# Five long products in place of 94 small unread ones at the start, and 56 small ones with one long one ahead of N

## The chip, the cores and the metric

The kernel runs on one core of a Trainium2 chip. The metric is the device time of one execution in microseconds; three runs of the kernel before took 701.88, 702.68 and 706.95 us (median 702.68). A separate execution was taken by the profiler; all durations below come from it.

## The reference

For 4 batches and 8 heads, a delta-rule recurrence over 768 tokens of 48 values each; its output, with the heads side by side (384 values a token), goes through a SwiGLU block with 1536 inner columns.

```
k_n = k / (norm(k) + 1e-6)
for t in range(S):
    y[t]  = q[t] @ state
    v_old = k_n[t] @ state
    state = state + beta[t] * outer(k_n[t], v[t] - v_old)
x = y as (B*S, H*D)                       # 3072 x 384
out = (silu(x @ w_gate) * (x @ w_val)) @ w_out
```

Everything is float32.

## The kernel before

The tokens are cut into 12 chunks of 64. Within a chunk the recurrence is turned into matrix products: the chunk's keys and queries are transposed on TensorE (`turned`, L497), Gram matrices of keys with keys and of queries with keys are formed (`first_gram`, L656 and L657, for the first two chunks; `gram_steps`, L513, for the rest), a triangular system is solved by substitution on VectorE, and `advance` applies the result to the values and to the running state (L899, L908, L938, L958, L994, L1006 and others). The feed-forward block of a finished chunk is worked off in between: L1270 for the first two chunks, L1174 for the others, L1380 for the output product. The products of the recurrence are small (64 or 32 rows, 48 to 64 columns) and come in groups of 64 and more; those of the feed-forward block are 128 x 128 with 128 to 256 columns. The order on every engine is written out by hand: the schedule is manual for TensorE, ACT, DVE, SP and POOL, and each engine works through its program in that order.

The change concerns the first chunk pair. Its order on TensorE is: `unread()`, then the transposes of chunk 0's keys, the first Gram, the transposes of chunk 1's keys, sixteen small products that spread beta (`spread_beta`, L438), the second Gram; then transposes and Grams for the first two query chunks and for key chunks 2 and 3. DVE meanwhile computes the norms and, once ACT has copied the second Gram's diagonal blocks (`first_diag`, L662) and DVE has transposed them (L1649), runs the first substitution (L698 and L704, until 27 us), from which `first_z` and `spread_z` (L708, L717, L719) make the tile `zt`. Then `warm(3)` (L644), three products of 512 columns that nobody reads, stands on TensorE ahead of N: `n_products` (L728), called by the first step of `advance(0)`, multiplies `zt` with the lower blocks.

`unread()` forms 94 products of a 32 x 32 block of the constant tile `half` with one column of it (L638); they go to a PSUM bank that nobody reads before it is written again. They wait only for the memset of `half` (L311). A float32 product shows up in the profile as two weight loads and two matmuls, so these are 188 and 188 instructions, and the three products of `warm(3)` are 6 and 6. Both functions take the pair of PSUM banks with the tag "px", which the key Grams of chunks 0 and 2 use too.

Of the kernel before, what the change touches and what calls it, by code (L numbers as in the profile page):

```python
# [15 lines left out]
R = 32  # L16
# [4 lines left out]
def kernel(  # L21
# [25 lines left out]
    nc = tc.nc  # L47
# [21 lines left out]
    def ps_pair(name, tag):  # L69

        return psum.tile([128, 2, 512], FP32, name=name, tag=tag, bufs=1)
# [70 lines left out]
    def load_k(c, dmas=(nc.sync,)):  # L142
        load_heads(kn_of(c), k, c, dmas)

    def load_q(c):
        load_heads(qpad[c % QB], q, c)
# [28 lines left out]
    def load_v(c):  # L175
        vin[c] = work.tile([128, 2, NB, NJ, D], FP32, name="vin", bufs=2)
        for b in range(2):
            src = halves(v, c, b).rearrange("bp (j par) p d -> par p (bp j) d", par=2)
            for par in range(2):
                s = 64 * (b ^ par)  # L180
                nc.sync.dma_start(
                    out=vin[c][s : s + 64, par].rearrange("p bp j d -> p (bp j) d"),
                    in_=src[par],
                )
# [125 lines left out]
    half = const.tile([128, R], FP32, name="half")  # L310
# [46 lines left out]
    def new_n(g):  # L357

        n_t[g] = work.tile([128, 2, HH], FP32, name="n_t")
# [58 lines left out]
    def load_beta():  # L418
        for s_ in range(2):
            for par in range(2):  # L420
                at = beta_rows(s_).start + 8 * par
                nc.gpsimd.dma_start(
                    out=beta_s[at : at + 8],
                    in_=beta.rearrange(
                        "(b bp) (j par) s -> b par (bp j) s", b=2, par=2
                    )[s_ ^ par, par],
                )
# [119 lines left out]
    def gram(*args):  # L547
        for _ in gram_steps(*args):
            pass
# [58 lines left out]
    def first_tiles():  # L608
        a = work.tile([128, C * 2 * HH], FP32, name="a_sb")
        for c in range(2):  # L610
            l_sb[c] = a[:, R * R * c : R * R * (c + 1)].rearrange(
                "p (h k) -> p h k", k=C
            )
        first_of["flat"] = new_mb().rearrange("p k i -> p (k i)")
        first_of["diag"] = first_of["flat"].rearrange("p (j h) -> p h j", j=R)
        first_of["zb"] = places["z1"].bitcast(FP32)[:, 4 * H_ - 1056 : 4 * H_]
        first_of["mb"] = places["wo"].bitcast(FP32)[:, 2 * H_ : 2 * H_ + 1056]
        nc.vector.memset(first_of["zb"], 0.0)
        for c in range(2):
            nc.vector.memset(l_sb[c][:, :, 48:C], 0.0)  # L620
        for x, rows in enumerate((slice(16, C), slice(R, C), slice(48, C), slice(0, R))):
            nc.vector.tensor_reduce(
                out=m_two[:, x],
                in_=ident.rearrange("p (b n) -> p b n", b=2)[:, :, rows],
                axis=mybir.AxisListType.X,
                op=ALU.add,
            )
        nc.vector.tensor_tensor(
            out=m_rows, in0=m_two[:, :, 0], in1=m_two[:, :, 1], op=ALU.add
        )  # L630
        nc.vector.tensor_scalar_mul(m_low, m_rows[:, 0:3], -1.0)

    def unread():

        p = ps_pair("p_t", "px")[:, 0]
        for n in range(94):
            q_ = QUADS[n % 4][0]
            nc.tensor.matmul(p[q_, 0:1], half[q_], half[q_, 0:1])  # L638

    def warm(count):  # L640

        p = ps_pair("p_t", "px")[:, 0]
        for _ in range(count):
            nc.tensor.matmul(p, ident, kts[0][:, 0:512])  # L644
# [15 lines left out]
    def first_diag(c, p):  # L660
        to = first_of["diag"][:, HH * c : HH * c + HH]
        nc.scalar.copy(to.rearrange("p (par h) j -> p par h j", par=2), p[:, :, 1])  # L662
# [957 lines left out]
    with tc.manual_schedule(  # L1620
        engines={
            mybir.EngineType.PE,
            mybir.EngineType.Activation,
            mybir.EngineType.DVE,
            mybir.EngineType.SP,
            mybir.EngineType.Pool,
        }
    ):
        new_n(0)
        load_beta()  # L1630
        first_tiles()
        norms(0)
        norms(1)
        load_q(0)
        load_k(2)
        load_k(3)
        load_q(1)
        load_v(0)
        copy_a = nc.scalar.copy
        unread()  # L1640
        turned(0, False, 0)
        p_g = [first_gram(0, "px")]
        first_diag(0, p_g[0])
        turned(1, False, 2)
        spread_beta(copy_a)
        p_g.append(first_gram(1, "py"))
        first_diag(1, p_g[1])
        r_b = first_n()
        nc.vector.transpose(first_of["mb"][:, 0 : R * R], first_of["flat"])  # L1649
        first_scale(r_b)  # L1650
        for n in range(12):
            stage(n, n - 2 if n > 1 else None)
        load_v(1)
        stage(12, 10)
        stage(13, 11)
        low_copies(0, p_g[0])
        turned(0, True, 0)
        low_copies(1, p_g[1])
        turned(2, False, "px")
        first_q = [gram_steps(0, True, 2)]  # L1660
        next(first_q[0])
        turned(3, False, "py")
        turned(1, True, 0)
        gram(2, False, "px", (copy_a, copy_a))
        gram(3, False, "py", (copy_a, copy_a))
        first_q.append(gram_steps(1, True, 0))
        next(first_q[1])
        for n in (0, 2):
            power_step(n)
        first_substitution()  # L1670
        for n in range(14, 18):
            stage(n, n - 3)
        first_z()
        for n in range(18, 23):
            stage(n, n - 3)
        some, others = slice(0, HH // 2), slice(HH // 2, HH)
        spread_z(0, 1, nc.scalar, some)
        spread_z(0, 0, nc.vector)
        spread_z(0, 1, nc.vector, others)
        scale_v(0)  # L1680
        for steps_of in first_q:
            next(steps_of)
        warm(3)
        new_nt(0, qpad[1].rearrange("p bp h d -> p (bp h d)"))
        zb_1 = work.tile([128, R, R], FP32, name="zb", bufs=1)
        new_nt(1, zb_1.rearrange("p k i -> p (k i)"))
        step("advance", advance, 0)
        for x in range(2):
            spread_z(1, x, nc.scalar)
        for n in (4, 1, 3, 5, 6, 7):  # L1690
            power_step(n)
        for _ in range(6):
            step("advance", advance, 0)
        converts_first(0)
        step("advance", advance, 0)
        converts_first(2)
        p_n = banks("p_n", "px")
        n_products(1, p_n, (0,))
        step("advance", advance, 0)
        converts_first(4)  # L1700
        n_products(1, p_n, (1,))
        converts_first(1, 3)
        converts_first(5)
        scale_v(1)
        for par in range(2):
            n_copy(1, p_n, par)

        def chain(at):

            step("advance", advance, 0 if steps("advance", 0) < 4 else 1)  # L1710
            converts(1 + (at + 1) % 2)

        pairs = [(c, f) for c in range(2) for f in range(0, 8, 2)]
        pairs += [(c, f) for f in range(8, FT, 2) for c in range(2)]
        for at, (c, f) in enumerate(pairs):
            early = c == 0 and f < 4
            if c == 1 and f == 0:
                finish(1)
                second_inverse.append(invert(1))
                for _ in range(3):  # L1720
                    next(second_inverse[0])
            elif not early:
                point(2)
            need((6, 12, 18, 24, 30, 30)[f // 2])
            gate_val(c, f, fill, at, chain if early else None)
        need(len(pieces))
        for bp in range(NB):
            point(2)
            output(0, bp, fill, (4, 8))
        output(1, 0, fill, (4, 8))  # L1730
        hold.clear()
        first_blocks(True)
        first_blocks(False)
        point(2)
        output(1, 1, fill, range(2, FT, 2))
        finish(2)
        x_sums(2)
        sums_of_w(12)
        for c in range(2, NCH):
            if c > FAST:  # L1740
                begin(c, 0)
            point(c + 1)
            if c == FAST:
                begin(c, 0)
            for r in range(ROUNDS):
                gate_val_fast(c, r, fill)
            output_fast(c, fill)
            finish(c + 1)
            x_sums(c + 1)
# [30 lines left out]
```

## Time and profile before

| | |
|---|---|
| three runs, median | 702.68 us |
| profiled execution, its own time | 704.07 us |
| its span, first to last instruction | 702.4 us |
| TensorE busy (matmul / weight load) | 684.1 / 643.0 us |
| VectorE, ScalarE, GpSimd busy | 473.0, 259.4, 54.0 us |
| mean granted TensorE clock in the records | 0.994 |
| first transposes (L497), first start | 5.71 us |
| N (L728), first start | 31.88 us |

The table's first three rows are times of whole executions: the profiled one took 1.7 us more than its span, and 1.4 us more than the median. Busy times are sums of instruction durations without their overlap. In the lines of the prediction, L followed by a number is a line of the kernel, PE stands for TensorE's matmuls and PEld for its weight loads; "idle before" names what ended the wait of an engine. "issue" is idle time for which the profile shows no other engine or transfer.

### The profile page before, as it was taken

The page shows a single profiled execution, that of the slowest core. Times are in us where ns is not written, and L with a number is a line of the kernel's source. Part 1 is how long each engine was busy: PE and PEld are TensorE (multiplying, and loading weights), DVE is VectorE, ACT ScalarE, POOL GpSimd, SP SyncE. Part 2 cuts the span into 40 slices and gives each one's busy share as a digit, 9 for nine tenths or more (in the row PEclk, how much of TensorE's full clock was granted, in tenths as well). Part 3 has the DMA queues.
Part 4 walks back from the last instruction along what each step waited for, and adds up shares of the span by engine and source line. Part 5 has one row for each costly group of instructions (what it writes and reads, how often), then busy time and mean ns, then how long its engine had stood idle before and what let it go on. Part 6 is the DMA issues. An engine that isn't in the chain of part 4 may idle for free.

```text
span 702.4 us, 25797 instructions
## 1 busy us (share of the span) xinstructions
PE 684.1 (97%) x11450; PEld 643.0 (92%) x11450; DVE 473.0 (67%) x1103; ACT 259.4 (37%) x542; POOL 54.0 (8%) x62
## 2 busy tenths in 40 slices
PE   6899999999999999999999999999999999999997
PEld 5788888757999989999999999999999999999997
DVE  6786788798899738887468787379844345333342
ACT  4674865214442523244223235232153132142220
POOL 4110031105000120000300000200000000000000
PEclk9999999999999999999999999999999999999999
DMA  8578724017450621365333264143241131221210
GB/s 133 155 183 210 215 85 141 4 37 174 126 108 13 118 69 46 77 130 91 75 84 72 56 133 88 31 117 84 55 107 48 42 84 59 55 62 46 68 46 23
DMA packets 143855, 62.33 MB, mean 89 GB/s; under 512 B 122976, under 2 KB 126048, under 8 KB 143744
## 3 DMA queue, kind: packets, MB, share of 16 engines
q1 hardware_dynamic: 141536, 60.19, 36.3%
q8 instruction: 90, 1.47, 0.8%
q10 hardware_dynamic: 2080, 0.39, 0.4%
q0 software_dynamic: 128, 0.10, 0.1%
q14 instruction: 21, 0.17, 0.1%
HBM read 53.58 MB, written 7.08 MB: 86 GB/s over the span
## 4 chain that ended last, share of the span: by engine, by line
PE 95%; ACT 2%; issue 1%; DVE 1%; DMA 1%; ACTq 0%; DVEq 0%
PE ffn L1174 43%; PE ffn L1380 20%; PE ffn L1270 9%; PE ffn L1297 4%; PE p_g L513 3%; PE p_u L938 2%; PE p_r L899 2%; PE p_s L1006 2%; PE p_y L908 2%; PE p_y L994 1%; PE p_f L1067 1%; PE p_u L958 1%; PE ffn L958 1%; PE ffn L497 1%; PE p_j L876 1%
## 5 line engine op out<-in xcount | busy, mean ns | idle before, releaser
L1174 PE MATMUL ffn<-x_ffn,wg_sb 128*128 128x128 f32 x840 | 128.9, 276 | 0.4 <-ACT x_ffn L1073 0.2
L1174 PE MATMUL ffn<-x_ffn,wv_sb 128*128 128x128 f32 x840 | 128.5, 276 | 0.0
L1174 PEld LDWEIGHTS ffn<-x_ffn,wg_sb 128*128 128x128 f32 x840 | 111.7, 193 | 0.6 <-ACT ffn L1230 0.3
L1174 PEld LDWEIGHTS ffn<-x_ffn,wv_sb 128*128 128x128 f32 x840 | 111.1, 193 | 0.1
L1204 ACT ACTIVATE sil<-ffn 128x256 f32<-128x256 f32 x120 | 46.1, 384 | 133.6 <-PE ffn L1174 125.3
L1380 PE MATMUL ffn<-wo_sb,h_f 128*128 128x192 f32 x480 | 83.4, 327 | 0.0
L1209 DVE TENSOR_TENSOR h_f<-sil,ffn 128x256 f32<-128x256 f32 x120 | 49.6, 418 | 49.5 <-ACT sil L1204 47.2
L1380 PEld LDWEIGHTS ffn<-wo_sb,h_f 128*128 128x128 f32 x480 | 78.1, 190 | 0.4
L1341 DVE TENSOR_TENSOR ffn<-ffn,p_sb 128x512 f32<-128x512 f32 x58 | 40.3, 695 | 44.3 <-ACT ffn L1230 43.2
L1174 PE MATMUL ffn<-x_t,h_f 128*128 128x128 f32 x480 | 61.0, 280 | 0.2 <-ACT ffn L1187 0.2
L1174 PEld LDWEIGHTS ffn<-x_t,h_f 128*128 128x128 f32 x480 | 56.2, 191 | 1.4 <-ACT ffn L1187 0.4
L591 DVE TENSOR_TENSOR zb<-zb,tmp 128x31 f32<-128x31 f32 (+15 forms) x155 | 53.1, 343 | 5.3
L585 DVE TENSOR_TENSOR tmp<-zb,mb 128x31 f32<-128x31 f32 (+15 forms) x155 | 52.7, 340 | 4.0
L807 POOL TENSOR_TENSOR n_b<-mb,half 128x32 f32<-128x32 f32 x5 | 30.0, 6003 | 294.6 <-DVE mb L555 294.6
L1341 DVE TENSOR_TENSOR o_sb<-o_sb,ffn 128x192 f32<-128x192 f32 x49 | 17.2, 352 | 51.2 <-PE ffn L1380 49.1
L1187 ACT COPY ffn<-ffn 128x512 f32<-128x512 f32 x30 | 17.1, 571 | 63.7 <-PE ffn L1174 57.3
L1380 PE MATMUL ffn<-last_k,h_f 128*128 128x192 f32 x200 | 35.9, 327 | 0.0
L1270 PE MATMUL ffn<-x_ffn,wg_sb 128*128 128x256 f32 x144 | 34.4, 385 | 0.0
L1270 PE MATMUL ffn<-x_ffn,wv_sb 128*128 128x256 f32 x144 | 33.8, 382 | 0.0
L1380 PEld LDWEIGHTS ffn<-last_k,h_f 128*128 128x128 f32 x200 | 32.9, 190 | 0.0
L1174 PE MATMUL ffn<-x_ffn,p_sb 128*128 128x128 f32 x216 | 30.9, 287 | 0.0
L1270 PEld LDWEIGHTS ffn<-x_ffn,wg_sb 128*128 128x128 f32 x144 | 26.5, 190 | 4.4 <-DVE wg_sb L304 0.8
(289 smaller groups left out, 1070.0 us busy)
## 6 DMA issues: line engine op xcount, KB each, us to landing
h_f<-w_s SPq DMA_DIRECT2D x60, 256.0 KB, 2.7
p_sb<-w_s SPq DMA_DIRECT2D x27, 256.0 KB, 2.9
vin<-in_v_dram SPq DMA_DIRECT2D x48, 96.0 KB, 3.0
out_dram<-o_sb SPq DMA_DIRECT2D x48, 96.0 KB, 2.2
kn<-in_k_dram SPq DMA_DIRECT2D x20, 192.0 KB, 4.8
zt<-in_moe_w_out_dram SPq DMA_DIRECT2D x6, 384.0 KB, 3.7
qpad<-in_q_dram SPq DMA_DIRECT2D x36, 64.0 KB, 2.9
w_s<-h_f SPq DMA_DIRECT2D x7, 256.0 KB, 4.3
```

The source lines that it names most:

```text
L513: nc.tensor.matmul(p_v[par][half_of(b if of_q else b ^ par), bp, j], kt[c][half_of(par), bp, j, b], xt[half_of(par), bp, j, b],)
L585: nc.vector.tensor_tensor(out=t_v, in0=zb[:, 0 : j + 1, j : j + 1].to_broadcast([128, j + 1, m]), in1=mb[:, j : j + 1, j + 1 : R].to_broad ...
L591: nc.vector.tensor_tensor(out=zb[:, 0 : j + 1, j + 1 : R], in0=zb[:, 0 : j + 1, j + 1 : R], in1=t_v, op=ALU.add,)
L807: nc.gpsimd.tensor_tensor(out=n, in0=mb.rearrange("p j i -> p (j i)")[:, 0 : R * R : R + 1], in1=half, op=ALU.pow,)
L1174: nc.tensor.matmul(p[:, u], w(u), moving, start=start and u == 0, stop=True, skip_group_check=True,)
L1187: nc.scalar.copy(p_y, p_x)
L1204: nc.scalar.activation(sil[:, n].rearrange("p (i n) -> p i n", i=2), p[:, 0:2], ACTF.Silu)
L1209: nc.vector.tensor_tensor(out=h_of(c, f, j), in0=sil[:, n].rearrange("p (i n) -> p i n", i=2), in1=p[:, 2:4], op=ALU.mult,)
L1270: nc.tensor.matmul(ps[name][:, i], w_sb[:, t, (f + i) * 128 : (f + i + 1) * 128], xts[c][:, t], start=(t == 0 and i == 0), stop=(t == KT - 1),
L1297: nc.tensor.matmul(p_o, hs[c, f - f % 2][:, f % 2, bp * 128 : (bp + 1) * 128], wo_sb[:, f], start=(f == 0), stop=(f == FT - 1),)
L1341: nc.vector.tensor_tensor(out=out, in0=a, in1=b, op=ALU.add)
L1380: nc.tensor.matmul(p[x, part], a(f - f % 2)[:, f % 2], b(f), start=not begun and f == 0, stop=f == FH - 1, skip_group_check=True,)
```

## The change

`unread` gets a count and forms products of the whole 128 x 32 tile `half` with one of its columns broadcast to 512; it is called with 5. The old small products become `small_unread(count)`, called with 56 behind the first query Grams. `warm` is called with 1 instead of 3. Nothing else is different.

```diff
-    def unread():
+    def unread(count):
 
         p = ps_pair("p_t", "px")[:, 0]
-        for n in range(94):
+        for _ in range(count):
+            nc.tensor.matmul(p[0:R], half, half[:, 0:1].to_broadcast([128, 512]))
+
+    def small_unread(count):
+
+        p = ps_pair("p_t", "px")[:, 0]
+        for n in range(count):
             q_ = QUADS[n % 4][0]
             nc.tensor.matmul(p[q_, 0:1], half[q_], half[q_, 0:1])
...
-        unread()
+        unread(5)
         turned(0, False, 0)
...
         for steps_of in first_q:
             next(steps_of)
-        warm(3)
+        small_unread(56)
+        warm(1)
         new_nt(0, qpad[1].rearrange("p bp h d -> p (bp h d)"))
```

## The prediction, made before the changed kernel ran

> **What bounds the kernel now.** I read the page's engine table and its chain first: is there any engine but TensorE to gain from?
>
> ```profile
> PE 684.1 (97%) x11450; PEld 643.0 (92%) x11450; DVE 473.0 (67%) x1103; ACT 259.4 (37%) x542; POOL 54.0 (8%) x62
> PE 95%; ACT 2%; issue 1%; DVE 1%; DMA 1%; ACTq 0%; DVEq 0%
> q8 instruction: 90, 1.47, 0.8%
> ```
>
> TensorE carries the end; what the change can touch is its idle time, the "issue" share and its clock. Next the waits of TensorE's matmuls from 33 us on, after the edited start:
>
> ```profile
> PE p_j L876 <- issue: 2.4, 2, 1.6
> PE p_y L908 <- issue: 1.2, 1, 1.2
> PE p_y L994 <- issue: 0.8, 1, 0.8
> ```
>
> The three longest sums are put down to no engine. Then TensorE's timeline in the edited stretch (start, length, instructions; in brackets the idle time before and what ended it), and one line of the chain there:
>
> ```profile
> 1.03 2.98 PE L638 MATMUL p_t<-half 32*32 32x1 f32 x188 [1.03 <-DVE half L311]
> ...
> 28.38 0.80 PE L513 MATMUL ffn<-qt,kt 64*64 64x64 f32 x35 [1.90 <-issue]
> 29.11 2.84 PE L644 MATMUL p_t<-kt,ident 128*128 128x512 f32 x6
> ```
>
> ```profile
> 31.95 1.14 PE p_n L728 x64
> ```
>
> 94 small products are 188 loads and 188 matmuls; they end at 4.01, and the first real work (L497) starts at 5.71, when its keys land. The three long products (L644) stand directly ahead of N (L728). Last, the view by windows around the longest late stall (stretch, length, busy time of TensorE, weight load, DVE, ACT and POOL, then clock, DMA share, GB/s):
>
> ```profile
> 248.59:250.15 1.56, 0.00 (x1) 0.00 (x0) 0.00 (x0) 0.00 (x0) 1.42 (x2) 1.00 0.00 0
> 250.62:254.03 3.41, 3.41 (x17) 3.41 (x18) 1.22 (x1) 0.96 (x1) 0.00 (x0) 0.50 0.18 53
> ```
>
> TensorE stands for 1.56 us; the next 3.41 us run at clock 0.50.
>
> To find what "issue" is I numbered TensorE's records by start. The stalls that end at 13.33, 28.38, 51.44, 165.49, 170.04, 245.05, 250.15 and 349.53 all fall on number 193 modulo 256. Queue q8 brings 90 packets of 16 KB, and 90 x 256 is 23,040, about TensorE's 23,053 records: q8 is its program. At each of these stalls the next block starts 1.3 to 1.5 us after its packet ends (packet 25.95 to 26.89, restart 28.38), and nowhere in the trace sooner. So **TensorE stalls for its own instructions** where a run of small products eats 256 instructions (2.0 to 3.6 us) faster than a block arrives: the packet starts 0.9 to 2.3 us after the previous block is entered, takes 0.9 to 1.5, and needs another 1.4.
>
> **What the Trainium skill says.** "Runtime: NRT & Kernel Launch", section Instruction fetch mechanics: blocks of 16 KiB (256 instructions) are fetched by the sequencer's own DMA queue, the cost "mostly hidden". The block size agrees; the hiding fails here for 1 to 2 us at a time. "TensorE: Matmul & The Clock Gate", Part 1: the array runs at half rate until a window of some 3.4 us was busy, and falls back after an idle one; the windows run freely. The trace agrees: a 128-column transpose takes a median 421 ns from 5.7 to 11.5 us and 272 at 22 us; the clock records begin with full at 11.69, and half windows last 3.41 us (18.51, 250.62). The page's clock of 1.00 before 11.69 is the absence of a record.
>
> **The change part by part.** No step of another engine moves: SP, POOL, ACT and DVE issue the same instructions and DMAs. TensorE's program changes in length.[...] Out: 94 x 4 = 376. In: 5 x 4 = 20, then 56 x 4 = 224. Of `warm`, 12 become 4. Up to the small ones everything is 356 earlier in the program, from N on 140.
>
> *Start.* At full clock L644's matmuls start 0.45 us apart (29.11 to 31.36, five steps). At half clock L497 took 1.94 us for 8 matmuls against 1.03, a factor 1.9: 0.85 us apart. Ten from 1.03 on end at 9.5 if the clock never rises. If 3.4 us of them count as a busy window, it rises between 4.4 and 7.85, by the phase; then they end at 1.03 + 4 x 0.85 + 6 x 0.45 = 7.1 up to 8.75. With this trace's phase (11.69 less 2 x 3.413 = 4.86): 7.3. They block L497, ready at 5.71, and all behind it on TensorE: **1.4 to 3.0 us late**. At full clock it regains 0.9 in each of two groups of transposes (1.94 and 1.85 against 1.03) and some 0.7 in the first Gram (7.6 to 10.0): 2.5. But the first block that must be fetched now begins 104 instructions into the second Gram; its fetch starts only when the first Gram is half done (about 9.8) and lands at 9.8 + 1 to 2 + 1.4 + 1.4 = 13.6 to 14.6. The last 152 instructions (6.7 ns each: 256 took 1.7 us from 13.33) end the Gram at 14.6 to 15.6 against 15.04. DVE's L1649, which waits for its copy, could start no earlier than 14.92 anyway, when DVE ends L453. Sum: **0** (from -0.6 to +1.2).
>
> *Before N.* The stall from 26.48 lay inside the second query Gram. The boundary is now 40 instructions into the small ones, so the Gram ends unstalled near 26.6 and the stall, until about 28.3, falls into filler. 184 small instructions at 7.9 ns (376 in 2.98 us) take 1.45, the long one 0.9: N at 30.7 instead of 31.9. Its values (`zt`, L717 and L719) are there from 29.2. But the next boundary lies 68 instructions into N; its block, asked for at 28.3, is there at 31.7 to 32.6. N then ends at 32.2 to 33.1 against 33.08: **-0.5** (-2 to +1; the upper end if small products don't hold the clock and a half window, 1.7, follows). The bank px, which the small ones take first, was read last by L539, done at 27.2: no new wait. If the filler were too short, N would wait for `zt`, 29.2.
>
> *Boundaries after N.* They move by 140 instructions. Gaps at old boundaries after 33 us: 1.40, 0.14, 0.34, 0.98, 0.32, 1.75, 1.05 = 6.0 us. I took these out of the trace's starts and replayed the fetches ([...]request to packet constant, 1.0 for the packet, 1.4 to use). With 1.6 us to the packet it returns 4.5 us on the old boundaries, at six of those seven places and a few others; on the new ones **2.3**. With 1.3: 1.1 and 0.8; with 2.0: 9.7 and 4.9; with latencies drawn from the trace's own 4.8 and 3.2. I take 3 left of 6: **-3.0** (-5 to +1). TensorE's waits for other engines after 33 us are 0.7 us at most, so little is swallowed.
>
> *Clock.* No new boundary lies between 240 and 259. Without the 1.56 us stall the window to 250.62 should hold enough work, and 3.41 us at half clock give back half: **-1.7** (0 if the small joins alone starve the window).
>
> Sum: 0 - 0.5 - 3.0 - 1.7 = -5.2. The profiled execution took 704.07 (span 702.4 and 1.7 around it): 698.9. The median shown, 702.68, is 1.4 below that execution: 697.5. **I forecast 698.0.**
>
> **The rivals.**
> *More is gained.* Fetches are quick after 33 us and hardly any stall is left, and the start gains too: -6.0 - 1.7 - 2.0 = -9.7, 693. For it: with 1.3 us to the packet the replay leaves only 0.8. Against it: near 35, 42 and 159 the replay finds new fast blocks while the weights' DMAs load the queues.
> *The stalls only move.* As much stall elsewhere, and a half window after another join: only -0.5 is left, 702. For it: the later joins (L876) are just such runs of small products. Against it: after 27 us, 28 blocks last under 5 us without stalls on the old boundaries, 22 on the new.
> *Slower: the long products stay cold.* Their stationary is 32 columns wide; if such work doesn't raise the clock, they hold L497 until 9.5. From L497 to the end of the second Gram took 9.3 us with its 0.7 stall; 9.5 + 8.6 = 18.1 against 15.04, +3.1, and DVE's substitution carries it to N. With stalls that only move: 705.8; with two more half windows, 709 or more. It decides once they end later than about 8.5.
> *No effect*, the filler being hidden: excluded by the shifted program for the late stalls, but possible in sum, as in the second rival.
>
> **Numbers.** Main case 0.55 (694.5 to 701); more gained 0.25; stalls only move 0.12; cold 0.08. Within 1% (7 us) is what a measurement of this kernel can't tell from no change. Faster by more: the second case and some of the main one, 0.40; same 0.53; slower 0.07. Range 693 to 704: it leaves out about 0.1 on each side.
>
> **What would show it.** Right: L638 with five products ending near 7 to 8; transposes near 280 ns right after; the "issue" stall behind L513 gone from that line and standing in the small products; stalls of L876, L908 and L994 smaller; no half clock after 250. Wrong: transposes still at 421 ns; L497 later than 9; stalls of 1 to 2 us at other lines with the same sum; a half window at 32.

## The result, and the profile after

The changed kernel took 698.88 us (median of 20 runs, 696.57 to 703.43), the kernel before 702.65 us (20 runs, 699.65 to 706.95): a ratio of 0.995, 95% interval 0.9932 to 0.9967. Its profiled execution took 697.91 us over a span of 696.2, against 704.07 over 702.4 before. So the gain is 3.8 us by the medians and 6.2 us between the two profiles; where the other 2.4 us went is taken up below.

From the profile's page of the kernel after: the busy time of each engine, the shares of the chain that ended last, and the queue that carries TensorE's program:

```profile
PE 684.1 (98%) x11380; PEld 638.6 (92%) x11380; DVE 473.2 (68%) x1103; ACT 259.4 (37%) x542; POOL 53.3 (8%) x62
PE 96%; ACT 1%; issue 1%; DVE 1%; ACTq 0%; DVEq 0%
q8 instruction: 89, 1.46, 0.8%
```

TensorE has 70 matmuls and 70 weight loads fewer, 140 instructions, and its program comes in 89 packets instead of 90. Its busy time is the same to a tenth of a microsecond, but by coincidence: up to 33 us it is busy for 27.75 us where it was 25.19, the five long products alone taking 6.62 us for the 2.98 of the 94 small ones, so behind 33 us it is busy for 2.6 us less. The waits of its matmuls from 33 us on (line, waited for: us in total, times, longest):

```profile
PE ffn L964 <- ACT v L953: 0.6, 1, 0.6
PE ffn L964 <- issue: 0.5, 1, 0.5
PE p_t L497 <- ACT x_ffn L1079: 0.4, 1, 0.4
PE p_y L914 <- issue: 0.4, 1, 0.4
PE ffn L1180 <- ACT ffn L1236: 0.2, 1, 0.2
PE p_j L791 <- issue: 0.2, 1, 0.2
```

The lines have moved by 6 (L876 of before is L882, L908 is L914, L994 is L1000). The 2.4 us at the join (L876) and the 0.8 at L994 are gone, the 1.2 at L908 is 0.4. Numbered as in the prediction, the gaps at block boundaries after 33 us sum to 2.4 us, against 6.1 in the kernel before (a gap is the time from the start of one record to the start of the next; those over 0.12 us that end within 1.8 us of a packet's end count). The largest now are 0.68 at 35.85 and 0.62 at 162.70.

Seen by windows, the two stretches where the long late stalls stood (stretch, length, then busy time and instructions of TensorE, weight load, DVE, ACT and POOL, clock, DMA share, GB/s), first before:

```profile
240.00:260.00 20.00, 18.39 (x489) 17.71 (x488) 9.94 (x17) 5.82 (x11) 6.33 (x2) 0.91 0.34 75
345.00:365.00 20.00, 19.14 (x448) 18.53 (x448) 10.26 (x21) 5.97 (x11) 4.74 (x3) 1.00 0.37 89
```

and after:

```profile
240.00:260.00 20.00, 20.00 (x564) 19.50 (x566) 11.10 (x21) 6.98 (x13) 6.58 (x3) 1.00 0.40 92
345.00:365.00 20.00, 20.00 (x451) 19.48 (x450) 12.34 (x28) 6.21 (x13) 0.24 (x1) 1.00 0.33 79
```

TensorE is busy throughout and its clock is full. A half window below is a stretch of 3.41 us for which the records show a clock of 0.50. To see where the time came from I set the records of the two traces side by side by their number counted from the end of the program. The same work is 0.8 us earlier in the kernel after at 55 us, 1.0 at 158, level at 165, 1.5 earlier from 180 to 242, 5.1 at 259, 6.2 from 362 to the end. Between 242 and 259 us 3.6 us are gained in one place: the stalls there (0.32 and 1.75 in the kernel before) and the half window behind them.

The edited stretch, on TensorE's timeline of the kernel after:

```profile
1.03 6.62 PE L637 MATMUL p_t<-half 128*32 128x512 f32 x10 [1.03 <-DVE half L311]
7.58 1.09 PE L497 MATMUL ffn<-ident,kn 128*128 128x128 f32 x8
...
25.88 0.29 PE L644 MATMUL p_t<-half 32*32 32x1 f32 x14
27.67 0.97 PE L644 MATMUL p_t<-half 32*32 32x1 f32 x98 [1.49 <-issue]
28.73 1.59 PE L650 MATMUL p_t<-kt,ident 128*128 128x512 f32 x2
30.25 2.49 PE L734 MATMUL p_n<-zt,a_sb 64*64 64x64 f32 x62
```

Five long products end at 7.6, and the transposes behind them run at full clock: 8 in 1.09 us where they took 1.94. The stall that stood in the query Gram now stands in the small products. N starts 1.6 us earlier than before, but takes 2.5 us instead of 1.2: a block boundary lies in it, and nearly all of it falls into a half window from 29.26 to 32.67 us. The copies behind it (L739) start at 32.87 against 33.11. So the change leaves as many half windows as there were: ahead of the end of the program the profile before has them at 18.51 and 250.62, the one after at 15.61 and 29.26, and the mean granted clock is 0.994 in both. The first 33 us by windows, before and after (the third number from the end is the clock):

```profile
0.00:33.00 33.00, 25.19 (x846) 21.11 (x850) 25.64 (x74) 16.34 (x32) 10.59 (x29) 0.95 0.76 145
0.00:33.00 33.00, 27.75 (x795) 18.85 (x796) 25.31 (x74) 16.37 (x33) 11.06 (x29) 0.90 0.77 137
```

### The profile page after: what moved, and what is told of

The parts are those of the page before. It is cut to its first block, busy times and chain, and to the rows that moved or that the text cites. A ratio compares the mean times of both kernels' runs of the same rounds, so it can differ in the third digit from the quotient of the medians.

```text
span 696.2 us, 25657 instructions
## 1 busy us (share of the span) xinstructions
PE 684.1 (98%) x11380; PEld 638.6 (92%) x11380; DVE 473.2 (68%) x1103; ACT 259.4 (37%) x542; POOL 53.3 (8%) x62
## 3 DMA queue, kind: packets, MB, share of 16 engines
q8 instruction: 89, 1.46, 0.8%
## 4 chain that ended last, share of the span: by engine, by line
PE 96%; ACT 1%; issue 1%; DVE 1%; ACTq 0%; DVEq 0%
PE ffn L1180 43%; PE ffn L1386 20%; PE ffn L1276 9%; PE ffn L1303 4%; PE p_g L513 3%; PE p_u L944 2%; PE p_s L1012 2%; PE p_r L905 2%; PE p_y L914 2%; PE p_y L1000 1%; PE p_f L1073 1%; PE p_t L637 1%; PE ffn L964 1%; PE p_u L964 1%; PE p_j L868 1%
## 5 line engine op out<-in xcount | busy, mean ns | idle before, releaser
L1180 PEld LDWEIGHTS ffn<-x_ffn,wv_sb 128*128 128x128 f32 x840 | 110.7, 192 | 0.0
L1276 PEld LDWEIGHTS ffn<-x_ffn,wv_sb 128*128 128x128 f32 x144 | 27.0, 190 | 3.7
```

What stands on the lines that cost most here:

```text
L1180: nc.tensor.matmul(p[:, u], w(u), moving, start=start and u == 0, stop=True, skip_group_check=True,)
L1276: nc.tensor.matmul(ps[name][:, i], w_sb[:, t, (f + i) * 128 : (f + i + 1) * 128], xts[c][:, t], start=(t == 0 and i == 0), stop=(t == KT - 1),
```

## The experiments

The theory: the gain comes from where the 256-instruction blocks of TensorE's program begin. The rivals: the early warm-up of the clock, the shorter filler ahead of N, or simply fewer instructions. None of the kernels below changes what is computed. Ratios are to the kernel before, timed on the same chip in the same session, with 95% intervals; "late stalls" are gaps at block boundaries after 33 us in one profile of the kernel. Each timed run also has its mean granted clock. Over the 120 runs of the kernel before in these sessions it averaged 0.9945; 0.001 of it is at most 0.7 us of 702.

**The boundaries alone, first try.** The kernel before with more small products:

```diff
-        for n in range(94):
+        for n in range(123):
```

> The kernel before with 123 small unread products in place of 94; nothing else. The 29 more (116 TensorE instructions, 0.9 us) fit into the wait for the keys, which ends at 5.7. From N on the block boundaries of TensorE's program then fall on the same instructions as in the changed kernel, with no warm-up and the three long products as before. Theory (the stalls for instructions are what moved): stalls at block boundaries after 33 us sum to 2 to 3.5 us, not 6.3; no half window after 250; 3 to 5 us faster than before. Rival (the early warm-up of the clock or the shorter filler is the gain): within 1 us of before, and if anything slower, for there are more instructions to fetch.

Measured: 701.62 us, ratio 0.9955 (0.9941 to 0.9969). Late stalls are 1.6 us, and nothing is left at 250; from 55 us to the end the same work gained 5.9 us on the kernel before. But it was 4.2 us late at 55 us. Its timeline (L638 is the small products; the first line begins where the view was cut, inside their run) shows why:

```profile
2.83 1.64 PE L638 MATMUL p_t<-half 32*32 32x1 f32 x101
8.30 0.49 PE L638 MATMUL p_t<-half 32*32 32x1 f32 x23 [3.83 <-issue]
8.72 1.97 PE L497 MATMUL ffn<-ident,kn 128*128 128x128 f32 x8
```

The first block that has to be fetched begins with record 449. 94 small products end ahead of it; with 123, the last dozen are behind it and wait until 8.30, and the first transposes with them. So my claim that 29 more products hide in the wait for the keys was wrong, for the very reason that the theory gives.

**The boundaries alone, second try.**

```diff
-        for n in range(94):
+        for n in range(59):
```

> The kernel before with 59 small products in place of 94: 140 instructions fewer, so that from N on every boundary falls where it falls in the changed kernel, and the first fetched block (number 449) begins in the first Gram and not, as with 123 products, ahead of it. Theory: with the boundaries alone the whole gain is there: late stalls of 2 to 3.5 us, no half window after 250, 4 to 6 us faster than before. Rival (123 products brought only part of the gain because warm-up and filler carry the rest): about 2.7 us faster, as with 123.

Measured: 698.59 us, ratio 0.992 (0.9899 to 0.9941), with late stalls of 3.0 us. One number, in products that nobody reads, brings as much as the whole change (0.9932 to 0.9967; the intervals overlap). Part of it may be clock: the six runs averaged 0.9983, against 0.9948 for the kernel before in that session, which is worth at most 2.5 us of the 6.1 gained. Its waits from 33 us on:

```profile
PE ffn L958 <- issue: 0.7, 1, 0.7
PE p_y L908 <- issue: 0.7, 1, 0.7
PE ffn L958 <- ACT v L947: 0.7, 1, 0.7
PE p_y L994 <- issue: 0.4, 1, 0.4
```

L876 is gone from the list, as in the kernel after.

**The change with the boundaries of before.** In the changed kernel:

```diff
-        small_unread(56)
+        small_unread(27)
```

> The changed kernel with 27 small products ahead of N in place of 56: 116 instructions fewer, so that from N on the block boundaries fall on the same instructions as in the kernel before. Theory: the stalls of before come back at the same places (L876, L914, L1000), 5 to 6.5 us in sum, perhaps with a half window after 250; within 1.5 us of before, although 0.9 us of filler is gone. Rival (warm-up or filler is the gain): as fast as the changed kernel or up to 0.9 us faster.

Measured: 705.36 us, ratio 1.0019 (1.0001 to 1.0037). Late stalls are 7.6 us. The warm-up is there, the filler is even shorter, the instructions are fewer, and the gain is gone. TensorE's waits from 33 us on:

```profile
PE p_u L944 <- issue: 1.8, 3, 0.7
PE p_j L882 <- issue: 1.8, 2, 1.0
PE p_y L914 <- issue: 0.7, 1, 0.7
```

The join (L882) is back. But this kernel has a handicap that isn't a late stall: its clock is at half for 10.24 us from 29.07 on, where the changed kernel has 3.41 us, and its runs averaged 0.991. From 29 to 39 us, the changed kernel first:

```profile
29.00:39.00 10.00, 8.76 (x264) 7.10 (x265) 6.00 (x11) 6.93 (x15) 1.43 (x5) 0.83 0.49 145
29.00:39.00 10.00, 8.19 (x200) 7.88 (x202) 4.70 (x9) 5.99 (x12) 1.52 (x6) 0.50 0.56 161
```

What comes after 55 us is free of that. From there to the end the same work gained, on the profile before, 5.4 us in the changed kernel, 5.9 with 123 products and 4.6 with 59, but 0.8 here; and 0.9 and 1.2 in the next two kernels, whose late boundaries are also those of before. So the late gain goes with the boundaries, with and without the warm-up and the shorter filler. That decides against these two rivals, and 123 products, which are more instructions and yet faster, against the third. In the profile before, about 1.7 us of that late gain is the half window behind 250 us; none of these six kernels has one there.

**The warm-up alone.** The kernel before, with 30 products of 85 columns at its start: the array time of five long ones, all boundaries as before, one block fewer.

```diff
-        for n in range(94):
-            q_ = QUADS[n % 4][0]
-            nc.tensor.matmul(p[q_, 0:1], half[q_], half[q_, 0:1])
+        for _ in range(30):
+            nc.tensor.matmul(p[0:R, 0:85], half, half[:, 0:1].to_broadcast([128, 85]))
```

> The kernel before with the 94 small products replaced by 30 of 85 columns (2550 columns where 5 of 512 have 2560, and 120 instructions, 256 fewer than 376), so that the clock is warmed up as in the changed kernel while every later boundary falls on the instructions of before. Theory: transposes at 280 ns from about 7.5 us on, late stalls of 5.5 to 6.5 us as before, time within 1.5 us of before. Rival: 3 to 4 us faster, as the changed kernel.

Measured: 703.91 us, ratio 0.9997 (0.9984 to 1.001); the transposes start at 7.54 and take 1.09 us for eight; late stalls 7.4 us. The warm-up alone brings nothing in sum.

**The filler alone.** The changed kernel with a start like that of before, with 104 small products so that the boundaries from N on fall as before:

```diff
-        unread(5)
+        small_unread(104)
```

> The changed kernel with 104 small products at the start in place of the five long ones: the filler ahead of N is that of the changed kernel, the start is that of before with 10 more small products, and from N on the boundaries fall on the instructions of before (416 + 224 + 4 is 256 more than 376 + 12). Theory: late stalls of 5 to 6.5 us; N starts 0 to 1 us earlier than in before; within 1.5 us of before. Rival (the shorter filler is the gain): 3 us or more faster than before.

Measured: 707.88 us, ratio 1.0045 (1.0027 to 1.0062): slower than expected. The 8.2 us of late stalls hold one of 2.87 at the boundary ahead of N (33.33 us), so that 5.3 are left for the later ones, as forecast. Besides, its profile is at half clock for 10.24 us from 14.38 and again from 34.86, and its runs averaged 0.9895, at most 3.5 us against 0.9945. The rival fell further than the theory, but the theory's own number was too small by about 2 us: it had neither that stall nor the clock.

**The change without its warm-up.**

```diff
-        unread(5)
+        small_unread(5)
```

> The changed kernel with five small products of one column in place of the five long ones at the start: the same 20 instructions, no warm-up. Theory (the start gains what it loses): transposes at half clock from 5.7 us, N within 1 us of the changed kernel, time within 1 us of it, late stalls as in it. Rival (the warm-up is worth its 2.5 us): 2 to 3 us slower than the changed kernel, about 701.5 where that takes 699.

Measured: 699.05 us, ratio 0.9932 (0.991 to 0.9954); the changed kernel had 0.995. The first transposes are early and at half clock,

```profile
5.80 1.94 PE L497 MATMUL ffn<-ident,kn 128*128 128x128 f32 x8 [4.41 <-DMA kn<-in_k_dram]
```

and DVE's transpose, with which the substitution begins, is a microsecond earlier without the long products than with them. DVE's timeline without them, then with them:

```profile
15.98 1.25 DVE L1655 STREAM_TRANSPOSE wo_sb<-mb 128x1024 f32<-128x1024 f32 x1 [1.30 <-ACT mb L668]
```

```profile
16.98 1.25 DVE L1655 STREAM_TRANSPOSE wo_sb<-mb 128x1024 f32<-128x1024 f32 x1 [2.27 <-ACT mb L668]
```

**The start cut finer.** The changed kernel with 60 products of 43 columns for its five of 512, so that the block of the second Gram is fetched earlier.

```diff
-            nc.tensor.matmul(p[0:R], half, half[:, 0:1].to_broadcast([128, 512]))
+            nc.tensor.matmul(p[0:R, 0:43], half, half[:, 0:1].to_broadcast([128, 43]))
...
-        unread(5)
+        unread(60)
```

> The changed kernel with its five products of 512 columns cut into 60 of 43 (2580 columns): the same array time, 220 instructions more, so that all boundaries move by 220 instructions (36 later in the work from N on, as with 47 small products). Theory: the block that the second Gram waits for in the changed kernel (2.04 us at 14.8) is fetched while the unread products run, and that stall shrinks to under 1 us; late stalls as with 47 small products. 1 to 3 us faster than the changed kernel. Rival (the start is set by DVE's norms and the copies): the second Gram ends earlier but N doesn't start earlier; within 1 us of the kernel with 47 small products.

Measured: 699.94 us, ratio 0.9931 (0.991 to 0.9951). The stall of 2.04 us at block 449 fell to 0.28, but the next boundary stalled for 2.69 us at 16.09, and late stalls were 5.3 us. No gain that the intervals can tell from the changed kernel: the stall moved.

**Another shift, as the replay would have it.** The changed kernel with 47 small products for 56.

```diff
-        small_unread(56)
+        small_unread(47)
```

> The changed kernel with 47 small products ahead of N in place of 56: 36 instructions fewer, so that all boundaries from there on fall 36 instructions later in the work; 0.3 us of filler goes. Theory: the stalls depend on where the boundaries fall; the replay of the fetches on the trace of before gives 0.8 us (1.6 us to the packet) or 2.3 us (drawn latencies) of stall after 33 us here, against 2.3 and 3.2 for the changed kernel: 0.5 to 2 us faster than the changed kernel, 4 to 7 us faster than before. Rival (the gain is the filler and the warm-up, the stalls are chance): as the changed kernel, 3.5 to 4.5 us faster than before.

Measured: 701.00 us, ratio 0.9948 (0.9926 to 0.9971), as the changed kernel and not better. Late stalls are 4.1 us: 1.46 at 53.19 and 0.79 at 68.62, and 0.9 in two near 166, where the replay had 0.8 us in all (2.3 with drawn latencies). The replay takes one time from request to packet for all blocks; that it was too short between 33 and 80 us, where the weights are loaded and the DMA share of the kernel before is 0.82, is likely and not shown.

**A shift that the replay calls worse.** The kernel before with 86 small products.

```diff
-        for n in range(94):
+        for n in range(86):
```

> The kernel before with 86 small products in place of 94: 32 instructions fewer, the start otherwise the same. Theory: the replay of the fetches gives 6.0 us of late stalls (1.6 us to the packet) where it gives 4.5 for the kernel before, the largest near 250 and 447 us: 0 to 2.5 us slower than before. Rival (fewer instructions are always better): 0.3 us faster or the same.

Measured: 703.36 us, ratio 0.998 (0.9969 to 0.9991): a little faster, not slower. Its late stalls, 7.2 us, are more than the 6.1 of before, as the replay said (1.06 at 249.68, 1.12 at 444.82). Yet in its profile no half window follows the stall near 250, and that is 1.7 us. Its runs averaged a clock of 0.9964 against 0.9948 for the kernel before in that session: at most 1.1 us of the 1.3 gained. Over the 120 runs of the kernel before, 0.001 of clock goes with only 0.27 us of time, which would make it 0.4 us. So the clock explains part of it, and how much isn't shown; the expectation missed.

**More columns in the filler.** The changed kernel with 16 columns in its small products.

```diff
-            nc.tensor.matmul(p[q_, 0:1], half[q_], half[q_, 0:1])
+            nc.tensor.matmul(p[q_, 0:16], half[q_], half[q_, 0:16])
```

> The changed kernel with small products of 16 columns in place of one: the same instructions, the same boundaries, more work in the array. Theory A (a stretch of one-column products counts as idle for the clock, which causes the half window at 29.3 us in the changed kernel): that half window is gone, 0.5 to 1.7 us faster than the changed kernel. Theory B (the half window there comes from the stall for instructions alone): it stays, and the time is that of the changed kernel within 0.7 us.

Measured: 699.24 us, ratio 0.9932 (0.9909 to 0.9955), and a half window from 28.4 us is still there. Sixteen columns don't remove it, so theory A isn't borne out; whether they are enough work for the clock no run shows. That the stall in the filler alone makes it isn't shown either: it is absent from the kernel without the long products, with a stall of 1.93 us at the same place.

**No filler.** The kernel before with 62 small products and without the three long ones ahead of N (140 instructions fewer).

```diff
-        for n in range(94):
+        for n in range(62):
...
-        warm(3)
+        warm(0)
```

> The kernel before with 62 small products in place of 94 and without the three long ones ahead of N: 140 instructions fewer, as with 59 products, with the same boundaries from N on. Theory: N then waits for its values (29.2 us in the kernel before) and starts 0 to 2.5 us earlier than with 59 small and three long products, unless a half window follows from the idle array: between 1 us slower and 2.5 us faster than that kernel.

Measured: 697.92 us, ratio 0.991 (0.989 to 0.9931), the lowest of all; late stalls 2.4 us. N starts at 30.34, when `zt` is there (its last part is written until 30.29), against 30.90 with 59 small and three long products. Against those (0.992) the difference can't be told; against the changed kernel (0.995, up to 0.9967) the intervals just part, in different sessions.

**No filler, with the warm-up.** The same with its 62 products 41 columns wide.

```diff
-        for n in range(62):
-            q_ = QUADS[n % 4][0]
-            nc.tensor.matmul(p[q_, 0:1], half[q_], half[q_, 0:1])
+        for _ in range(62):
+            nc.tensor.matmul(p[0:R, 0:41], half, half[:, 0:1].to_broadcast([128, 41]))
```

> The kernel with 62 small products and no filler, its small products widened to 41 columns of the whole tile (2542 columns, as five of 512): the same instructions and the same boundaries, with the warm-up of the changed kernel. Theory (the start gains what it loses): the clock is full from 5 to 8 us on, L497 starts 1.4 to 3 us later, and the time is within 1.5 us of the kernel with 62 small products, 0.989 to 0.993 of before. Rival (the warm-up is worth its 2.5 us where no stall eats it): 0.987 to 0.988 of before.

Measured: 700.32 us, ratio 0.9932 (0.9908 to 0.9956). The clock is full from 4.96 us and L497 starts at 7.61, but a stall of 2.06 us stands at 14.92 in the second Gram, and from 28.85 on the clock is at half for 10.24 us, where the kernel without the warm-up has one half window (30.23). Its runs averaged 0.990 against 0.996 there. The warm-up brings nothing here either. The rival was the warm-up where no stall eats it, and a stall was there, so what it would bring without one stays untested.

## Why the prediction was right, point by point

*Total.* Forecast 698.0, measured 698.88, a gain of 3.8 us by the medians where 5.2 was summed up. The mechanism was right: stalls for instructions moved, and fewer are left. That the total came so near is in part luck, for the stalls gave more than was put down for them and the clock nothing that the timed runs show. Nor was 1% the limit of what can be told from no change: the interval of the ratio is 0.0035 wide.

*Start, 0 (from -0.6 to +1.2).* The long products ended at 7.6 us (7.3 said for that phase) and DVE's L1655 started 0.87 us later than before (16.98 against 16.11):

```profile
16.11 1.25 DVE L1649 STREAM_TRANSPOSE wo_sb<-mb 128x1024 f32<-128x1024 f32 x1 [1.19 <-ACT mb L662]
```

That is inside the range, on its losing side. The reason was the one given: the block of the second Gram became usable at 14.79 (13.6 to 14.6 said), a stall of 2.04 us. The warm-up alone (0.9997) and the change without it (0.9932) agree that it is worth nothing in sum.

*Before N, -0.5.* The stall moved from the Gram into the filler and ended at 27.67 (28.3 said); N started at 30.25 (30.7 said); the copies behind N gained 0.24 us. The boundary in N and the half window, both named, took most of it; the half window was also listed as a sign of being wrong. One reading failed: `zt` was not there from 29.2 us on but, as the substitution had begun later, at 30.12. N started 0.13 us after that, at about the end of the long product (30.32); which of the two held it can't be told.

*Boundaries after N, -3.0.* The gaps went from 6.1 to 2.4 us, so -3.7. Shown by the pair of 59 products (gain with the boundaries alone) and 27 products (no gain with everything else), and by the work after 55 us: the seven kernels with the new late boundaries gained 3.3 to 5.9 us there on the profile before, the three with the old ones 0.8 to 1.2. With the 0.24 us ahead of it and nothing for the clock, the 3.7 come near the 3.8 us of the medians.

*Clock, -1.7.* True of that place in the profiled pair: the half window after 250 us is gone, and that stretch gave the largest single step. But the change brought one of its own, in N. The 20 timed runs of the changed kernel averaged a clock of 0.9942, no more than the 0.9945 of the kernel before in the later sessions. So this term is not seen in the medians. The forecast took it from one profile. Two readings under it were wrong. There are new boundaries between 240 and 259 us, at 242.16, 247.91 and 257.64 on the clock of the profile before; what is true is that TensorE stalls at none of them. And the prediction has the clock fall back after an idle window; the one ahead of this half window was not idle: from 247.21 to 250.62 matmuls were busy for 1.85 of 3.41 us.

A stall at the join doesn't suffice. Four other kernels stalled there in their profiles (1.21 with 27 products, 0.66 with the warm-up alone, 0.93 with the filler alone, 1.06 with 86) and none fell to half clock; their windows with the stall were busy for 2.39, 2.94, 2.67 and 2.54 us. The stall of before was longer, and all of it lay within one window. That the rest of the 2.4 us between profiles and medians is of this kind is not shown: both profiles have the same mean clock.

*The method.* The replay was right on the direction between the two kernels, on the order of the sum (2.3 us left, 2.4 measured), and on places: it named fast blocks near 35, 42 and 159 us, and stalls stand at 35.85, 43.40 and 158.53. For single shifts it was not good enough to choose by (47 and 86 products). One of its inputs was read too low: at the eight stalls that the prediction lists, the packet starts 1.1 to 2.8 us after the first record of the block before, not 0.9 to 2.3.

## What to carry to other kernels

When idle time of the busiest engine is put down to nothing, number its instructions and look at the remainder by the block size of its program: here every such stall fell on one remainder. Runs of small instructions that eat a block faster than the next arrives pay for it where a boundary lies badly, so that adding or removing instructions that do nothing moves time hundreds of microseconds later. Judge an edit that changes the instruction count only beside a control with the same count modulo the block, or its own effect and the shift can't be told apart. Even such controls are not exact: the late stalls were 6.1 us in the kernel before and 7.4 and 7.6 in two kernels with the same late boundaries. And a gain that one profile shows in the clock is worth comparing with the granted clock of all timed runs before it is counted.

## What the runs showed of the hardware that wasn't expected

- The first block that TensorE's program has to wait for begins at record 449: with 123 small products TensorE stood 3.83 us in front of it, until 8.30 us, although the program had hardly begun.
- In all kernels looked at, a block was used no sooner than 1.2 us after its packet had ended, mostly 1.3 to 1.6.
- Products with a stationary tile of 32 columns and 512 or even 41 moving columns raised the clock: it was full from 5.36 us with 5 of 512 and from 4.96 with 62 of 41. With 123 products of one column, on which TensorE was busy from 1.03 to 4.47 us, eight transposes still took 1.97 us at 8.72, and the first record of full clock is at 21.55.
- The clock fell without an idle window. Cut into windows of 3.41 us counted from the clock records, the fourteen profiles have 19 windows of full clock before 680 us that are followed by one of half clock. Matmuls were busy for up to 0.60 of such a window (2.04 us from 32.33, with 59 products). No window that was busy for longer was followed by half clock, but neither were all those below (0.44 from 25.34 in the kernel before).
